# Agent attention with a gated convolution on one core: loads without a hold, twelve query units transposed by TensorE, another order of TensorE's steps

## The chip, the core and the metric

The kernel runs on one core of one Trainium2 chip, in one launch. The metric is the device time of that core in microseconds: the median of 3 runs of the kernel before is 424.46 us (422.56 to 425.1).

## What is computed

Four batches of 12800 rows and 128 channels, 49 agents per batch, all float32 at the interface. `sm` is a softmax over the last axis.

```python
a2k = sm(agents, k)              # scale = 1/sqrt(128) inside sm
agent_v = a2k @ v                # 49 x 128 per batch
x = sm(q, agents) @ agent_v      # 12800 x 128 per batch
gate_pre[:, s] = sum(conv_w[j] * xp[:, s + j] for j in range(5))   # xp: x with 4 zero rows ahead
out = (sigmoid(gate_pre) * (x @ w_val)) @ w_out
```

## The kernel before

**Units.** A batch is cut into 10 units of 1280 rows, so there are 40 units of k, 40 of v and 40 of q, and the query units are numbered 0 to 39 through all batches (unit 21 is q2.1). The output is cut into 25 chunks of 512 rows per batch, chunk 0 to 100 (the last 512 rows are two half chunks). Two query units make a segment of 2560 rows, which five chunks read: segment 11 is units 22 and 23, and chunk 55 is the first that reads it.

**Steps on TensorE.** `k` (a unit's key scores) and `q` (its query scores) are 16 fp32 matmuls of 320 columns each (L404). `v` multiplies a unit's exponentials with v, 40 fp32 matmuls of 129 columns (20 of 64 weights' columns in batch 0; L508). `t` transposes a query unit's weights. For a chunk there are `g` (five fp16 matmuls at L950 on the rows x1, and a sixth at L954 on x2), `a` (L977, L981) and `o` (three, L1020 to L1022), each of 512 columns. `m` and `f` are the few small steps that take a batch's maximum and fold its agent values with the weights of the gate, the value and the output. The text `order` (L1065 on) is a list of all these steps written out by hand, and TensorE does its steps in that order. Four PSUM accumulators stand beside it: two banks `sc`, in turn for k, q and the t that TensorE does, and one each for gate, val and out.

**A query unit's way.** After `q`, VectorE transposes in 32x32 blocks (L414, sT) and takes the maximum (L773), GpSimd subtracts it (L778, qw), ScalarE exponentiates (L786), VectorE sums, inverts and scales (L791, L792, L795, L800), and ScalarE (L807) and GpSimd (L813, L821) write the fp16 weights and their rests, `pt`, 128 rows by 10 blocks of 128. `pt` is one of 4 buffers. A transpose then brings `pt` into x1: units 0 to 3 by TensorE (ten transposes at L876, then ScalarE copies one half out of PSUM at L883 and VectorE the other at L888), the other 36 by a DMA transpose on SyncE's queue (L862). Two further DMAs per segment (L911, x<-x, of 60 and 35 rows) copy shifted rows of x1 into x2, once both units stand in x1.

**The DMA queue.** All loads, DMA transposes, x<-x copies and output stores are issued by SyncE, in one order, and each waits there for what it needs before the next is issued. A load (L397) takes one of 11 buffers `ld` in turn, so the load of a unit needs the buffer that the unit 11 places earlier in the list of k, v and q steps has used. Eight DMA semaphores are used in turn: a DMA is issued when the eighth before it has landed.

**The planner.** Every step is recorded with an engine, a planned duration, what it reads and writes (`Plan.add`, L79), and `Plan.order` (L92) replays the whole in a cost model and returns the order in which the instructions are emitted: on TensorE the order of the text, on the other engines and on the queue the ready step with the longest chain behind it. It replays twice. From the first replay it takes when the first user of each load starts, and in the second a load is held until HOLD = 13 us (planned) before that (`early`, L398; `hold`, L101).

Of the kernel before, what the change touches and what calls it, by code (L numbers as in the profile page):

```python
# [44 lines left out]
CUT = 2  # L45
NOB = 4
SINGLE = 4
PE_FIRST = 4
PE_TURNS = ()
TURN = 3  # L50
W_AT = 2
HOP = 0.07
GAP = {"act": 0.11, "dve": 0.1, "pool": 0.055}
SWITCH = 0.13
DRAIN = 0.16
LANES = 8
FIRST = 0.85
LAND = 0.95
MEET = 0.3
HOLD = 13.0  # L60
BEGIN = {"pe": 1.5, "act": 2.4, "dve": 1.6, "pool": 2.3, "dma": 1.2}

QS = 256.0
# [4 lines left out]
class Plan:  # L68
# [7 lines left out]
    def __init__(self):  # L76
        self.steps, self.wrote, self.read = [], {}, {}

    def add(self, engine, us, fn, reads=(), writes=(), moved=0.0, key=None, urge=0.0, early=None):  # L79
        i = len(self.steps)  # L80
        need = set()
        for x in reads:
            need |= self.wrote.get(x, set())
        for x in writes:
            need |= self.wrote.get(x, set()) | self.read.get(x, set())
        for x in reads:
            self.read.setdefault(x, set()).add(i)
        for x in writes:
            self.wrote[x], self.read[x] = {i}, set()
        self.steps.append((engine, us, fn, need, moved, key, urge, early))  # L90

    def order(self):  # L92
        self.replay({})
        users = {i: [] for i, s in enumerate(self.steps) if s[7] is not None}
        for j, s in enumerate(self.steps):
            for i in s[3]:
                if i in users:
                    users[i].append(self.start[j])
        return self.replay({i: min(users[i]) - self.steps[i][7] for i in users})

    def replay(self, hold):  # L101
        n = len(self.steps)
        after = [[] for _ in range(n)]
        last = None
# [6 lines left out]
                last = i  # L111
        tail = [0.0] * n
        for i in reversed(range(n)):
            engine, us, fn, need, moved, key, urge, early = self.steps[i]
            cost = us + HOP
            if engine == "dma":
                cost = FIRST + moved + LAND
            tail[i] = cost + urge + max((tail[j] for j in after[i]), default=0.0)
        engines = ("pe", "act", "dve", "pool", "dma")
        free = dict(BEGIN)  # L120
        wire = 0.0
        lanes = [0.0] * LANES
        left = [len(s[3]) for s in self.steps]
        at = [hold.get(i, 0.0) for i in range(n)]
        queues = {e: [] for e in engines}
        pe = [i for i, s in enumerate(self.steps) if s[0] == "pe"]
        here = 0
# [5 lines left out]
        done = 0  # L133
        while done < n:
            best = None
            free["dma"] = max(free["dma"], lanes[0])
            for e in engines:
                if e == "pe":
                    if here < len(pe) and not left[pe[here]]:
                        pick, when = pe[here], max(free[e], at[pe[here]])  # L140
                    else:
                        continue
                elif queues[e]:
                    q = queues[e]
                    soon = min(max(free[e], at[i]) for i in q)
                    open_ = [i for i in q if at[i] <= soon + 0.05]
                    pick = max(open_, key=lambda i: (tail[i], -i))
                    for i in q:
                        if tail[i] > tail[pick] + 1.0 and at[i] < soon + 0.6 * self.steps[pick][1]:
                            pick = i  # L150
                    when = max(free[e], at[pick])
                else:
                    continue
                if best is None or when < best[0]:
                    best = when, e, pick
            when, e, i = best
            engine, us, fn, need, moved, key, urge, early = self.steps[i]
            if e == "pe":
                here += 1
                if key != kind and {key, kind} & {"sc", "av"}:  # L160
                    when += SWITCH
                kind = key
                end = when + us + DRAIN + HOP
                free[e] = when + us
            elif e == "dma":
                queues[e].remove(i)
                free[e] = when + us
                busy = wire > when + FIRST
                wire = max(wire, when + FIRST) + moved
                if key == "t":  # L170
                    wire += MEET if busy else 0.0
                    free[e] = max(free[e], wire - moved)
                end = wire + LAND
                lanes = lanes[1:] + [end]
            else:
                queues[e].remove(i)
                end = when + us + HOP
                free[e] = when + us - GAP[e]
            start[i] = when
            done += 1  # L180
            for j in after[i]:
                if i in self.steps[j][3]:
                    left[j] -= 1
                    at[j] = max(at[j], free[e] if e == "pe" == self.steps[j][0] else end)
                    if not left[j] and self.steps[j][0] != "pe":
                        queues[self.steps[j][0]].append(j)
# [5 lines left out]
def tile_agent_attention_gated_conv(  # L192
# [10 lines left out]
    B, C, N = qT.shape  # L203
    A = 49
    NU = N // UNIT
# [11 lines left out]
    add = plan.add  # L217
# [8 lines left out]
    m2 = const.tile([P, 2], F32, name="m2")  # L226
# [155 lines left out]
    def load(kind, b, u):  # L382
        i = taken[0] % NLOAD
        taken[0] += 1
        slot_of[kind, b, u] = i
        if kind == "v":
            dst, src = ld[i], vP[b, u].rearrange("p n c -> p (n c)")
        else:
            dst = ld[i][:, 0:UNIT]
            src = (kT if kind == "k" else qT)[b, :, u * UNIT : (u + 1) * UNIT]  # L390
# [4 lines left out]
        for d, f, keys in parts:  # L395
            add(
                "dma", 0.46, lambda d=d, f=f: nc.sync.dma_start(out=d, in_=f), (), keys,  # L397
                1.65 * f.shape[1] / src.shape[1], early=HOLD,  # L398
            )

    def score_matmuls(b, src, out):
# [426 lines left out]

    def on_pe(b, u):
        g = b * NU + u  # L830
        return g < PE_FIRST or (g < (B - 1) * NU and g % TURN in PE_TURNS)

    def unit_rows(g):
        o = PAD + g % 2 * UNIT
# [224 lines left out]
    def step(fn, b):  # L1059
# [3 lines left out]

    kinds = {"m": "max", "f": "fold"}
    order = (  # L1065
# [24 lines left out]
    )  # L1090
    work = [(kinds.get(x[0], x[0]), *map(int, x[1:].split("."))) for x in order.split()]

# [67 lines left out]
```

## Time and profile before

| what | value |
|---|---|
| median of 3 runs | 424.46 us |
| the profiled execution | 428.87 us |
| its span, first to last instruction | 426.9 us |
| TensorE busy | 398.2 us, 93% of the span |
| VectorE, ScalarE, GpSimd busy | 305.1, 305.8, 236.5 us |
| share of the SP queue's packets in 16 DMA engines' span | 94.1% |
| DMA packets moved | 127.64 MB |

A busy TensorE counts modelled ends of pipelined matmuls, so the time of a step is read from the start of one to the start of the next. The DMA share is the time of all packets over that of 16 engines, and goes over 1 where packets of several DMAs are under way on an engine at once. Waits are put down to what came last.

### The profile page before, as it was taken

What the parts mean: (1) busy time and instruction counts of PE and PEld (TensorE: products, weight loads), DVE (VectorE), ACT (ScalarE), POOL (GpSimd) and SP (SyncE); (2) the same over time, 40 slices, a digit from 0 to 9 for tenths busy, and PEclk for the clock granted to TensorE, in tenths of its full rate; (3) what the DMA queues carried; (4) which work ended last, traced back from release to release, by engine and by line L of the source; (5) the groups of instructions that cost most, each with busy time, mean ns of one, the idle gap of its engine ahead of it and who ended that gap; (6) DMA issues with size and microseconds to landing.
All of it is one profiled execution on the core that took longest, in us unless ns stands there. A gap on an engine that the chain in (4) does not pass through costs nothing.

```text
span 426.9 us, 10123 instructions
## 1 busy us (share of the span) xinstructions
PE 398.2 (93%) x3907; PEld 199.7 (47%) x3907; DVE 305.1 (71%) x570; ACT 305.8 (72%) x524; POOL 236.5 (55%) x303
## 2 busy tenths in 40 slices
PE   5869989997999999999989999999989999999996
PEld 2329534455454443464734444446564444444443
DVE  5988879776887778569658978486475887777221
ACT  7657347895658767997648677689826778778876
POOL 2510236454467635755756455674462879886653
PEclk9998999999999999999999999999998999999999
DMA  8999997999999999999999999979999778496733
GB/s 320 419 370 415 391 323 243 343 349 418 318 258 283 340 325 228 371 405 232 399 231 350 346 348 280 267 267 319 343 388 219 249 209 288 96 335 201 205 134 138
DMA packets 75131, 127.64 MB, mean 299 GB/s; under 512 B 50466, under 2 KB 50978, under 8 KB 75084
## 3 DMA queue, kind: packets, MB, share of 16 engines
q1 hardware_dynamic: 74940, 126.87, 94.1%
q8 instruction: 31, 0.51, 0.5%
q10 hardware_dynamic: 144, 0.13, 0.2%
q14 instruction: 16, 0.13, 0.1%
HBM read 79.25 MB, written 26.21 MB: 247 GB/s over the span
## 4 chain that ended last, share of the span: by engine, by line
PE 56%; DMA 35%; DVE 4%; ACT 2%; issue 2%; SPq 1%; POOL 0%; ACTq 0%; DVEq 0%
PE gate L950 18%; DMA ld<-kT 16%; PE sc L404 11%; DMA x<-pt 8%; DMA ld<-vP 5%; PE val L977 4%; PE out L1020 4%; DMA x<-x 4%; PE val L981 4%; PE out L1021 4%; PE gate L954 4%; PE out L1022 4%; DMA ld<-qT 3%; PE av L508 3%; DVE h L990 1%
## 5 line engine op out<-in xcount | busy, mean ns | idle before, releaser
L1001 POOL TENSOR_TENSOR hl<-h,hh 128x512 f16<-128x512 f32 (+1 forms) x101 | 117.4, 1167 | 89.1 <-ACT hh L996 87.1
L950 PE MATMUL gate<-x,stat 128*128 128x512 f16 (+1 forms) x500 | 124.1, 378 | 0.7 <-ACT th L963 0.5
L990 DVE SCALAR_TENSOR_TENSOR h<-th,val 128x512 f32<-128x512 f32 x100 | 67.7, 677 | 69.6 <-PE val L981 35.7
L404 PE MATMUL sc<-ld,ag_sb 128*32 128x320 f32 x1280 | 99.4, 444 | 12.0 <-DMA ld<-qT 7.2
L963 ACT ACTIVATE th<-gate,unscale 128x512 f32<-128x512 f32 x100 | 68.3, 683 | 34.9 <-PE gate L954 33.0
L1034 ACT ACTIVATE ob<-out,oscale 128x512 f32<-128x512 f32 x98 | 67.2, 686 | 14.5 <-PE out L1022 14.3
L950 PEld LDWEIGHTS <-stat 128*128 128x128 f16 x505 | 48.4, 98 | 59.9 <-issue 6.3
L996 ACT CAST hh<-h 128x512 f16<-128x512 f32 (+1 forms) x101 | 61.5, 611 | 18.4 <-DVE h L990 17.2
L404 PEld LDWEIGHTS sc<-ld,ag_sb 128*32 128x32 f32 x1280 | 38.9, 111 | 62.2 <-issue 13.2
L778 POOL TENSOR_TENSOR qw<-sT,qmx 128x490 f32<-128x490 f32 x40 | 40.6, 1020 | 29.1 <-DVE qmx L773 28.7
L508 PE MATMUL av<-ld,eT 128*32 128x129 f32 (+1 forms) x1400 | 49.6, 276 | 4.8 <-DVE eT L414 2.4
L508 PEld LDWEIGHTS av<-ld,eT 128*32 128x32 f32 (+1 forms) x1400 | 46.2, 115 | 9.9 <-DVE eT L414 3.9
L813 POOL TENSOR_SCALAR pt<-qw 128x240 f16<-128x240 f32 x80 | 28.1, 373 | 31.8 <-DVE qw L800 31.8
L821 POOL TENSOR_TENSOR pt<-qw,pt 128x490 f16<-128x490 f32 x40 | 43.6, 1094 | 3.3 <-ACT pt L807 3.3
L497 ACT ACTIVATE e<-ks,kbias 128x320 f32<-128x320 f32 x80 | 39.4, 554 | 6.5 <-DVE eT L414 6.1
L414 DVE STREAM_TRANSPOSE sT<-sc 128x640 f32<-128x640 f32 x40 | 33.6, 844 | 13.9 <-PE sc L404 12.7
L430 ACT COPY ks<-sc 128x640 f32<-128x640 f32 x40 | 27.4, 689 | 21.8 <-PE sc L404 19.2
L414 DVE STREAM_TRANSPOSE eT<-e 128x640 f32<-128x640 f32 x40 | 33.3, 839 | 12.6 <-PE av L508 7.6
L954 PE MATMUL gate<-x,stat 128*128 128x512 f16 x100 | 38.0, 380 | 3.7 <-DMA x<-x 3.7
L977 PE MATMUL val<-x,stat 128*128 128x512 f16 x100 | 38.1, 381 | 1.4 <-DVE h L990 1.3
L981 PE MATMUL val<-x,stat 128*128 128x512 f16 x100 | 38.0, 380 | 0.0
L1020 PE MATMUL out<-hh,wo 128*128 128x512 f16 x98 | 37.5, 383 | 0.0
(133 smaller groups left out, 428.4 us busy)
## 6 DMA issues: line engine op xcount, KB each, us to landing
ld<-qT SPq DMA_DIRECT2D x40, 640.0 KB
ld<-kT SPq DMA_DIRECT2D x40, 640.0 KB
ld<-vP SPq DMA_DIRECT2D x39, 645.0 KB
outT<-ob SPq DMA_DIRECT2D x48, 512.0 KB
x<-x SPq DMA_DIRECT2D x18, 300.0 KB
x<-x SPq DMA_DIRECT2D x18, 175.0 KB
outT<-ob SPq DMA_DIRECT2D x3, 256.0 KB
x<-x SPq DMA_DIRECT2D x4, 150.0 KB
```

What stands on the lines that cost most here:

```text
L404: nc.tensor.matmul(out=out[g * BLK : (g + 1) * BLK, j, 0:GT], lhsT=ag_sb[:, b, j * BLK : (j + 1) * BLK], rhs=src[:, g * GT : (g + 1) * GT] ...
L414: nc.vector.transpose(out=out.rearrange("p n (j i) -> p j n i", j=2), in_=in_.rearrange("p j (n i) -> p j n i", i=BLK),)
L508: nc.tensor.matmul(out=av[o + j : o + j + cols, 0 : C + 1], lhsT=et[:, n, j : j + cols], rhs=vt[:, n, :], start=(u == 0 and n < 2), stop=( ...
L950: nc.tensor.matmul(out=pg, lhsT=stat[:, k, :], rhs=x1[:, c : c + w], start=(k == 0), stop=False,)
L954: nc.tensor.matmul(out=pg, lhsT=stat[:, TAPS + 1, :], rhs=x2[:, o2 : o2 + w], start=False, stop=True,)
L963: lambda: nc.scalar.activation(out=th, in_=pg, func=AF.Tanh, scale=unscale[:, 0:1]),
L977: nc.tensor.matmul(out=pv, lhsT=stat[:, TAPS, :], rhs=x1s[(b * NCH + n0 // CH) // 5 % NX][:, PAD + o2 : PAD + o2 + w], start=True, stop=False,
L981: nc.tensor.matmul(out=pv, lhsT=stat[:, TAPS + 2, :], rhs=x2[:, o2 : o2 + w], start=False, stop=True,)
L990: lambda: nc.vector.scalar_tensor_tensor(out=h, in0=th, scalar=1.0, in1=pv, op0=ALU.add, op1=ALU.mult),
L996: "act", 0.19 + 0.42 * scale, lambda: nc.scalar.copy(out=hh, in_=h),
L1001: lambda: nc.gpsimd.tensor_tensor(out=hl, in0=h, in1=hh, op=ALU.subtract),
L1034: lambda: nc.scalar.activation(out=ob[:, o : o + w], in_=po, func=AF.Copy, scale=oscale),
```

## The change

Three things change. First, the hold: `early`, the first replay and `hold` are gone, so a load may be ordered as soon as its buffer is free; in place of the hold the cost model issues no DMA while the transfers already issued would take more than BACKLOG = 2.5 us (planned) from then. Nothing of BACKLOG is in the emitted program but the order. Second, TensorE also transposes units 6, 9, 12, 15, 18, 21, 24 and 27, beside 0 to 3; the queue has 28 DMA transposes instead of 36. Third, the text of TensorE's steps is another one. In it the k, v and q steps stand in 27 runs (before: 29) between fp16 steps, counting a `t` of TensorE as fp16.

```diff
-PE_FIRST = 4
-PE_TURNS = ()
-TURN = 3
+PE_UNITS = (0, 1, 2, 3) + tuple(range(6, 28, 3))
...
+BACKLOG = 2.5
...
-HOLD = 13.0
...
     def order(self):
-        self.replay({})
-        users = {i: [] for i, s in enumerate(self.steps) if s[7] is not None}
-        for j, s in enumerate(self.steps):
-            for i in s[3]:
-                if i in users:
-                    users[i].append(self.start[j])
-        return self.replay({i: min(users[i]) - self.steps[i][7] for i in users})
-
-    def replay(self, hold):
...
-        at = [hold.get(i, 0.0) for i in range(n)]
+        at = [0.0] * n
...
-            free["dma"] = max(free["dma"], lanes[0])
+            free["dma"] = max(free["dma"], lanes[0], wire - BACKLOG)
...
-                1.65 * f.shape[1] / src.shape[1], early=HOLD,
+                1.65 * f.shape[1] / src.shape[1],
...
-        return g < PE_FIRST or (g < (B - 1) * NU and g % TURN in PE_TURNS)
+        return g in PE_UNITS
...
-        "o5 a8 t0.7 k2.1 v1.2 v1.3 k2.2 v1.4 v1.5 k2.3 v1.6 q0.9 o6 g11 o7 a9 t0.8 t0.9 g12 a10 "
-        "o8 k2.4 q1.0 o9 a11 q1.1 q1.2 v1.7 v1.8 v1.9 o10 a12 g13 a13 f1 o11 g14 a14 t1.0 t1.1 "
+        "g16 o11 a14 g17 q1.1 v1.2 v1.3 q1.2 t1.1 v1.4 q1.3 k2.1 v1.5 v1.6 v1.7 v1.8 v1.9 k2.2 "
+        "k2.3 o12 a15 g18 t1.2 o13 a16 f1 g19 o14 a17 f1 g20 o15 a18 g21 o16 k2.4 k2.5 k2.6 k2.7 "
...
+        "g39 o34 a37 g40 t1.9 q2.1 v2.8 k3.3 v2.9 q2.2 o35 t2.0 a38 g41 o36 f2 a39 t2.1 g42 o37 "
```

Lines after the first are 11 lower in the changed kernel (L404 is L393, L414 is L403, L862 is L851, L911 is L900).

Place one, SyncE's queue around the DMA transpose of unit 23 (q2.3; it reads pt3 and writes x1_3) and the x<-x copies of segment 11 (they write x22, which is x2 buffer 2). Before:

```order
L862 DMA_TRANSPOSE x1_3_104<-pt2_99 128x10x128
L911 DMA x21_106<-x1_2_103 60x1x2560
L911 DMA x21_106<-x1_2_103 35x1x2560
L862 DMA_TRANSPOSE x1_3_104<-pt3_100 128x10x128
L1049 DMA outT<-ob1_121 128x1024
L397 DMA ld8_69<-qT 128x1280
L911 DMA x22_107<-x1_3_104 60x1x2560
L397 DMA ld9_70<-qT 128x1280
L911 DMA x22_107<-x1_3_104 35x1x2560
```

And in the changed kernel:

```order
L1038 DMA outT<-ob2_122 128x1024
L386 DMA ld10_71<-qT 128x1280
L386 DMA ld0_61<-qT 128x1280
L386 DMA ld1_62<-qT 128x1280
L386 DMA ld2_63<-vP 128x1290
L386 DMA ld3_64<-vP 128x1290
L386 DMA ld4_65<-vP 128x1290
L386 DMA ld5_66<-vP 128x1290
L851 DMA_TRANSPOSE x1_3_104<-pt3_100 128x10x128
L386 DMA ld6_67<-vP 128x1290
L386 DMA ld7_68<-vP 128x1290
L900 DMA x22_107<-x1_3_104 60x1x2560
```

Seven loads (q2.8 to v3.3) now stand straight ahead of that transpose and two more between it and the copies; before, none of the three places ahead of it was a load, and one load stood ahead of the copies.

Place two, VectorE between the block transpose (sT1) and the scaling (qw1) of unit 21, the unit whose `t2.1` TensorE now does. Before:

```order
L414 STREAM_TRANSPOSE sT1_86<-sc0_134 128x2x10x32
L414 STREAM_TRANSPOSE sT0_85<-sc1_135 128x2x10x32
L990 SCALAR_TENSOR_TENSOR h2_113<-th2_110,val_137 128x512
L773 TENSOR_REDUCE qmx1_88<-sT1_86 128x10
L773 TENSOR_REDUCE qmx0_87<-sT0_85 128x10
L990 SCALAR_TENSOR_TENSOR h0_111<-th0_108,val_137 128x512
L990 SCALAR_TENSOR_TENSOR h1_112<-th1_109,val_137 128x512
L791 TENSOR_REDUCE qsm1_94<-qw1_90 128x10
L792 SCALAR_TENSOR_TENSOR qsm1_94<-qsm1_94,tiny_146 128x10
L795 RECIPROCAL qr1_96<-qsm1_94 128x10
L990 SCALAR_TENSOR_TENSOR h2_113<-th2_110,val_137 128x512
L800 TENSOR_TENSOR qw1_90<-qw1_90,qr1_96 128x490
```

And in the changed kernel:

```order
L403 STREAM_TRANSPOSE sT1_86<-sc0_134 128x2x10x32
L762 TENSOR_REDUCE qmx1_88<-sT1_86 128x10
L780 TENSOR_REDUCE qsm0_93<-qw0_89 128x10
L781 SCALAR_TENSOR_TENSOR qsm0_93<-qsm0_93,tiny_146 128x10
L784 RECIPROCAL qr0_95<-qsm0_93 128x10
L789 TENSOR_TENSOR qw0_89<-qw0_89,qr0_95 128x490
L536 COPY av2_165<-av_139 128x129
L780 TENSOR_REDUCE qsm1_94<-qw1_90 128x10
L781 SCALAR_TENSOR_TENSOR qsm1_94<-qsm1_94,tiny_146 128x10
L784 RECIPROCAL qr1_96<-qsm1_94 128x10
L789 TENSOR_TENSOR qw1_90<-qw1_90,qr1_96 128x490
```

The maximum of unit 21 now follows its transpose at once, and what stands between is the scaling of unit 20 (qw0) and the copy of a batch's agent values, in place of four steps of chunks (h) and another unit's two.

## Rows read from the trace of the kernel before

**Rows 1.** The page: span, and section 1 (busy us, share of the span, instructions).

```profile
span 426.9 us, 10123 instructions
PE 398.2 (93%) x3907; PEld 199.7 (47%) x3907; DVE 305.1 (71%) x570; ACT 305.8 (72%) x524; POOL 236.5 (55%) x303
```

**Rows 2.** Busy time of each engine in stretches (start:end, length, then busy us and instructions of PE, PEld, DVE, ACT, POOL; the last three columns are granted clock, DMA share, GB/s).

```profile
40.00:420.00 380.00, 367.46 (x3554) 182.27 (x3551) 273.10 (x512) 274.64 (x478) 224.32 (x279) 1.00 0.95 292
20.00:40.00 20.00, 15.05 (x202) 10.85 (x196) 16.12 (x31) 13.34 (x26) 1.83 (x4) 0.91 1.02 392
60.00:80.00 20.00, 18.88 (x158) 8.15 (x159) 16.23 (x27) 14.07 (x24) 12.28 (x15) 1.00 0.90 279
320.00:340.00 20.00, 18.88 (x106) 8.48 (x106) 12.80 (x31) 13.26 (x23) 10.04 (x13) 0.91 0.90 228
```

**Rows 3.** What TensorE waited for between 40 and 420 us (waiting line, releaser: us in total, times, longest).

```profile
PE gate L954 <- DMA x<-x: 3.7, 2, 3.0
PE av L508 <- DMA ld<-vP: 2.4, 4, 1.2
PE sc L404 <- DMA ld<-qT: 1.9, 4, 1.0
PE sc L404 <- DMA ld<-kT: 1.8, 3, 1.1
```

**Rows 4.** The time line, TensorE: its first scores, the ten v of batch 0, and its first gate matmuls (start, us, what; in brackets the idle time before and what ended it).

```profile
5.28 8.19 PE L404 MATMUL sc<-ld,ag_sb 128*32 128x320 f32 x80 [5.28 <-DMA ld<-qT]
...
32.58 12.90 PE L508 MATMUL av<-ld,eT 128*64 128x129 f32 x200 [2.42 <-DVE eT L414]
...
52.31 1.24 PE L950 MATMUL gate<-x,stat 128*128 128x512 f16 x5
```

**Rows 5.** The same between 84 and 94 us: fp16 steps, then v, two k, v, a q, then fp16 again.

```profile
85.15 0.38 PE L954 MATMUL gate<-x,stat 128*128 128x512 f16 x1
85.46 1.31 PE L508 MATMUL av<-ld,eT 128*32 128x129 f32 x40
86.58 2.34 PE L404 MATMUL sc<-ld,ag_sb 128*32 128x320 f32 x32
88.73 1.29 PE L508 MATMUL av<-ld,eT 128*32 128x129 f32 x40
89.83 1.26 PE L404 MATMUL sc<-ld,ag_sb 128*32 128x320 f32 x16
91.03 0.39 PE L1020 MATMUL out<-hh,wo 128*128 128x512 f16 x1
...
91.69 0.38 PE L977 MATMUL val<-x,stat 128*128 128x512 f16 x1
...
92.12 1.25 PE L950 MATMUL gate<-x,stat 128*128 128x512 f16 x5
...
93.42 0.38 PE L1020 MATMUL out<-hh,wo 128*128 128x512 f16 x1
```

**Rows 6.** The time line at the last `t` of TensorE, and two groups by line, TensorE's transposes and ScalarE's copies of them (busy us, mean ns of one, idle time before).

```profile
63.61 0.72 PE L876 MATMUL sc<-ident,pt 128*128 128x128 f16 x10
64.17 0.38 PE L977 MATMUL val<-x,stat 128*128 128x512 f16 x1
L876 PE MATMUL sc<-ident,pt 128*128 128x128 f16 x40 | 2.9, 219 | 0.9 <-POOL pt L821 0.7 <-ACT ks L430 0.2
L883 ACT COPY x<-sc 128x640 f16<-128x640 f16 x4 | 2.8, 691 | 0.9 <-PE sc L876 0.9
```

**Rows 7.** The time line of query unit 0 from its block transpose to TensorE's transposes.

```profile
7.69 0.85 DVE L414 STREAM_TRANSPOSE sT<-sc 128x640 f32<-128x640 f32 x1 [2.08 <-PE sc L404]
...
15.71 0.56 PEld L876 LDWEIGHTS <-pt 128*128 128x128 f16 x10 [1.27 <-POOL pt L821]
```

**Rows 8.** The DMAs: sizes by kind, and the DMA transposes as instructions on SyncE's queue (duration ns min/median/max, first and last start us).

```profile
ld<-kT SPq DMA_DIRECT2D x40, 640.0 KB
outT<-ob SPq DMA_DIRECT2D x48, 512.0 KB
x<-x SPq DMA_DIRECT2D x18, 300.0 KB
x<-x SPq DMA_DIRECT2D x18, 175.0 KB
L862 SPq DMA_TRANSPOSE x<-pt x36: 1342/2772/8391, 70.5 to 398.4; - x36
```

**Rows 9.** TensorE's time line at two of its waits for loads, q0.9 and q2.2.

```profile
106.86 1.28 PE L404 MATMUL sc<-ld,ag_sb 128*32 128x320 f32 x16 [0.23 <-DMA ld<-qT]
...
216.36 1.28 PE L404 MATMUL sc<-ld,ag_sb 128*32 128x320 f32 x16 [0.28 <-DMA ld<-qT]
```

**Rows 10.** SyncE's queue and TensorE around the longest wait for x<-x (segment 13, chunk 65).

```profile
298.97 5.08 SPq L862 DMA_TRANSPOSE x<-pt  x1
304.18 1.62 SPq L397 DMA_DIRECT2D ld<-vP  x3
305.90 1.28 SPq L1049 DMA_DIRECT2D outT<-ob  x2
309.09 1.69 SPq L911 DMA_DIRECT2D x<-x  x2
...
321.12 0.59 PE L954 MATMUL gate<-x,stat 128*128 128x512 f16 x1 [2.95 <-DMA x<-x]
```

More of the change, by code (lines that the diff above doesn't have):

```diff
@@ L77, in __init__, with add @@
         self.steps, self.wrote, self.read = [], {}, {}
-    def add(self, engine, us, fn, reads=(), writes=(), moved=0.0, key=None, urge=0.0, early=None):
+    def add(self, engine, us, fn, reads=(), writes=(), moved=0.0, key=None, urge=0.0):
         i = len(self.steps)
@@ L89, in add @@
             self.wrote[x], self.read[x] = {i}, set()
-        self.steps.append((engine, us, fn, need, moved, key, urge, early))
+        self.steps.append((engine, us, fn, need, moved, key, urge))
     def order(self):
-        self.replay({})
-        users = {i: [] for i, s in enumerate(self.steps) if s[7] is not None}
-        for j, s in enumerate(self.steps):
-            for i in s[3]:
-                if i in users:
-                    users[i].append(self.start[j])
-        return self.replay({i: min(users[i]) - self.steps[i][7] for i in users})
-    def replay(self, hold):
         n = len(self.steps)
@@ L113, in replay @@
         for i in reversed(range(n)):
-            engine, us, fn, need, moved, key, urge, early = self.steps[i]
+            engine, us, fn, need, moved, key, urge = self.steps[i]
             cost = us + HOP
@@ L156, in replay @@
             when, e, i = best
-            engine, us, fn, need, moved, key, urge, early = self.steps[i]
+            engine, us, fn, need, moved, key, urge = self.steps[i]
             if e == "pe":
```

43 rows, old and new, of the table order are left out of this document.

## The prediction

> **What bounds the kernel now.** I read the page first. TensorE is busy 93% of a span of 426.9 us, VectorE and ScalarE a little over 70% [rows 1]; so what TensorE waits for decides. The stretches come next: between 40 and 420 us TensorE is busy 367.46 of 380 us, which leaves 12.5 us idle, at a DMA share of 0.95 [rows 2]. Two things are full at once, and the question is what a relief of the queue gives back against what it costs TensorE.
>
> The list of waits says what ends the idle time: DMAs, 3.7 us for x<-x, 2.4 for v, 1.9 for q, 1.8 for k, together 9.8 of the 12.5 [rows 3]. After the 2.95 us wait for x<-x the granted clock is 0.91 over 320 to 340 us, where it is 1.00 before [rows 2, 10]: 0.09 of 20 us, 1.8 us more. So DMAs cost 11.6 us after the start, 6.1 for loads and 5.5 for x<-x.
>
> **Prices on TensorE.** From start to start a score step is 1.075 us (two in 2.15), v 1.10, g 1.30, a 0.43, o 0.66; entering an fp32 run costs 0.09 (0.31 from the last fp16 matmul, of which the matmul is 1.30/6), leaving one 0.12, together 0.21 [rows 5]. A v of batch 0 is 1.29 (ten in 12.90) [rows 4], a t of ten transposes 0.56 [rows 6]. The small steps m and f I put at 0.2 and 0.3. With these I can say how much work of its own TensorE has done ahead of any step, and compare it with its start: the first gate starts at 52.31 us [rows 4] after 35.8 us of work (17 scores, ten v, three t, six runs, some small steps), so TensorE trails its work by 16.5 us by then.
>
> **Prices in the queue.** A load is 640 KB, an output 512, the two x<-x of a segment 475 [rows 8]; in the stretch of 20 to 40 us, nearly all loads, 392 GB/s flow [rows 2]. That makes 1.67, 1.34 and 1.24 us. A DMA transpose has no such row: as an instruction on the queue it takes 1.34 us at least, 2.77 at the median [rows 8]. The minimum belongs to an empty queue and this one is full, so I take 2.77.
>
> **Why loads are late, and whether they still will be.** I add up what the queue has to move up to a load, and set it against TensorE's work ahead of the step that uses it. Before, q0.9: 51 loads, 2 transposes, 5 x<-x pairs (four of them of one unit, half as long) and 2 outputs make 97.1 us, against 85.3 us of work; the queue is 11.8 behind. It starts at 106.86 [rows 9], 21.6 behind its work, so a load is usable some 9.8 us later than the tally. q2.2: 85 loads, 13 transposes, 10 pairs and 15 outputs make 207.3, against 189.8; 17.5 behind. It starts at 216.36 [rows 9], 26.6 behind, so 9.1 later than the tally. The two agree. After the change the worst place past the start is k2.3, at the end of a run of 14 fp32 steps: 58 loads, 3 transposes, 6 pairs, 5 outputs, 116.9 us, against 109.9 of work. It asks for a trail of 7.0 + 9.8 = 16.8 us, and TensorE trails by about 16.5 from the start on. At q2.2, 87 loads, 10 transposes, 11 pairs and 16 outputs make 205.0, against 200.8: a trail of 14.0. So the order, more than the eight transposes, takes the loads' waits away, because chunks stand ahead of the scores that they used to follow. I take all 6.1 us; at worst none is saved.
>
> **x<-x.** The queue has one order, so a transpose waits behind loads that go out in a burst. Before, the transpose at 298.97 had three v loads and two outputs between it and its x<-x copies at 309.09, and these let TensorE go on at 321.12 [rows 10]. The hold had kept those loads back until that burst. Without it the burst comes where fp32 steps free buffers. At segment 11 seven loads (11.7 us), the transpose (2.77), two more loads (3.3) and the copies (1.24) follow the end of q2.3, 19.0 us, with 2.9 us more as the first load shows (first scores at 5.28, queue from 0.74 on, less 1.67) [rows 4]: 21.9, where TensorE has 25.2 us of steps up to chunk 55 (11 scores, five g, six a, five o, a t). At segment 14 eight loads, two transposes, an output and the copies, 21.5 + 2.9 = 24.4, stand against 25.7 from the end of v3.0 on (nine v, two scores, five g, six a, six o). I call both about even: half of the 5.5 us is saved, 2.75; the ends are all of it and none.
>
> **What TensorE gets.** Eight t more: 8 x 0.56 = 4.5 us. Two fp32 runs less, 29 to 27: -0.4. A t also waits for pt, with all of TensorE behind it. Unit 0 needs 8.0 us from its block transpose to TensorE's transposes, in a stage with little else, and TensorE's weight load had been idle 1.27 us for it [rows 7]. TensorE's own steps between q and t give 8.2 us for unit 21 and 9.4 for unit 27, the shortest, and 11 to 22 for the others; VectorE now scales unit 20 between, and does four h less. Ends: 0, and 8 x 1.27 = 10.2. I take 2.0, a wait at units 21 and 27 and little else.
>
> The copies out of PSUM, 0.69 us on ScalarE for each t [rows 6] and a like one on VectorE, I price at 0: both engines are idle over a quarter of the span [rows 1], and a unit's first chunk is 11 us or more behind its t. With that cover gone they would cost 8 x 0.69 = 5.5.
>
> **The start.** Loads of q0.3 and k1.0 now stand ahead of v0.9's, 2 x 1.67 = 3.3 us later, while TensorE does two scores and one t more ahead of its first gate, 2.7 us. I take 0; the ends are -2.7 and 3.3.
>
> **Sum.** 4.5 - 0.4 + 2.0 - 6.1 - 2.75 = -2.75 us. The profiled execution's span of 426.9 becomes 424.15. Its own time is 428.87, 2.0 over the span; the median is 4.4 us under that. Applied to the median, 424.46 - 2.75 = **421.7 us**.
>
> **A rule against the change.** Ten transposes of TensorE took 0.72 us together, the next matmul starting 0.56 after the first of them, and the granted clock of that stretch is 1.00 [rows 2, 6]. The Trainium skill, page "TensorE: Matmul & The Clock Gate", section "Part 4: PE-mode transpose", says a 128x128 transpose takes about 275 ns in a kernel, and that the clock's full rate does not engage for it. By that rule 80 more would be 22.0 us instead of 4.5, and the time 439.2. The trace does not agree with it: neither the spacing nor the clock shows it.
>
> **Rivals.**
> *x<-x late twice.* Both bursts jam as segment 13 did: 2 x (2.95 + 1.8) = 9.5 us in place of my 2.75, so 421.7 + 6.75 = 428.5, slower than before. It decides where a segment's copies land over 25.2 us after q2.3 (25.7 for segment 14). For it: one queue, and my margins of 3.3 and 1.3 us. Against: the copies are needed only by a gate's sixth matmul, 1.08 us on.
> *TensorE waits for pt.* All eight new t wait like the first one did: 10.2 instead of 2.0, so 429.9. For it: pt takes 8.0 us even in an empty stage. Against: six units have over 11 us, and the order on VectorE now favours these units.
> *The queue was the bound.* Both x<-x waits go and no t waits: -2.75 - 2.0 more, so 417.0. For it: the DMA share of 0.95. Against: burst places remain.
> *Transposes don't overlap.* Each costs the 219 ns of its own record [rows 6], 80 x 0.219 = 17.5 instead of 4.5, so 434.7. Against it stands the spacing of 56 ns.
>
> **Chances.** A measurement of this kernel can tell about 1% from no change: 420.2 to 428.7. Forecast 0.50, itself from 418.5 to 425, of which 0.18 lies under 420.2. Queue as the bound 0.19, all faster. x<-x late 0.17, of which 0.08 over 428.7 and the rest within 1%. pt late 0.13, 0.10 over. No overlap 0.01. Faster 0.18 + 0.19 = 0.37; slower 0.08 + 0.10 + 0.01 = 0.19; the rest, 0.44, within 1%. The range of 414.5 to 429.5 leaves out the low end of the queue's case (0.04) and the upper ends of the two late ones and the last (0.13).
>
> **What would show it.** TensorE's waits for ld loads after 40 us under 1 us in all; for x<-x two or three short ones at segments 11 and 14; at L865 idle time from GpSimd's pt near 2 us, most of it at units 21 and 27; DMA transposes 28; a DMA share under 0.95. I am wrong if loads still make TensorE wait for over 3 us (then the tally misses what blocks the queue), if the first gate starts over 3 us later than 52.31 with only the 2.7 us of work gained, or if ScalarE and VectorE take the place of the DMAs in the list of waits.

## The result and the profile after

The changed kernel takes 428.54 us (median of 20 runs, 425.55 to 432.39), the kernel before 425.15 us in the runs beside it (20 runs, 422.56 to 430.63). The ratio is 1.0079, with a 95% interval of 1.0058 to 1.0099: 0.8% slower, where 421.7 us, 0.65% faster, was forecast. The profiled executions took 432.35 us here and 428.87 before, each 3.7 to 3.8 us over its kernel's median.

The page of the changed kernel and its stretches, in the columns of [rows 1, 2] (start:end, length, busy us and instructions of PE, PEld, DVE, ACT, POOL, then granted clock, DMA share, GB/s):

```profile
span 430.6 us, 10315 instructions
PE 402.5 (93%) x3987; PEld 207.5 (48%) x3987; DVE 306.7 (71%) x578; ACT 311.3 (72%) x532; POOL 237.2 (55%) x303
...
q8 instruction: 31, 0.51, 0.5%
```

```profile
40.00:420.00 380.00, 366.37 (x3580) 186.71 (x3577) 274.44 (x521) 276.13 (x480) 222.12 (x275) 0.99 0.91 284
300.00:320.00 20.00, 15.65 (x403) 12.32 (x401) 11.77 (x20) 12.45 (x24) 6.19 (x8) 1.00 0.90 319
320.00:340.00 20.00, 18.17 (x116) 9.45 (x116) 15.53 (x38) 11.15 (x20) 11.35 (x15) 0.91 0.57 161
```

The span is 3.7 us longer. TensorE is idle for 13.6 us between 40 and 420, as it was before (12.5), although the DMA share has gone from 0.95 to 0.91. What it waits for is another thing, as its waits in that stretch show (us in total, times, longest):

```profile
PE av L497 <- issue: 9.7, 5, 3.0
PE gate L939 <- ACT th L952: 2.4, 6, 0.7
PE sc L393 <- DMA ld<-qT: 0.3, 1, 0.3
```

Against [rows 3], loads fall from 6.1 to 0.3 us and x<-x from 3.7 to nothing. In their place stand 9.7 us put down to "issue": nothing that the profile shows held TensorE. In the kernel before that was this line alone:

```profile
PE sc L404 <- issue: 0.2, 1, 0.2
```

All five are inside runs of v. The time line of v3.0 to v3.9, ten in a row, on TensorE:

```profile
304.47 3.73 PE L497 MATMUL av<-ld,eT 128*32 128x129 f32 x128
309.48 3.73 PE L497 MATMUL av<-ld,eT 128*32 128x129 f32 x127 [1.28 <-issue]
314.77 3.72 PE L497 MATMUL av<-ld,eT 128*32 128x129 f32 x126 [1.56 <-issue]
321.00 0.74 PE L497 MATMUL av<-ld,eT 128*32 128x129 f32 x18 [2.51 <-issue]
```

The breaks come every 126 to 128 matmuls. Each matmul has a weight load of its own, so that is some 256 instructions, and the page has a queue q8, kind "instruction": 31 packets of together 0.51 MB for 2 x 3987 = 7974 instructions of TensorE, 257 to a packet. At 1.10 us for 80 instructions a packet lasts 3.5 us; from break to break it took 5.0, 5.3 and 6.2. Ten v took 17 us instead of 11. The DMA view of 302 to 322 us has three such packets beside the loads (packets, MB, share of the 16 engines):

```profile
q1 hardware_dynamic: 1417, 6.32, 87.8%
q8 instruction: 3, 0.05, 0.8%
```

The single records of the trace tie the breaks to these packets. Ahead of the five breaks stand 2753, 4545, 6337, 6593 and 6849 records of TensorE, each 193 more than a multiple of 256, and each break ends 1.3 to 1.5 us after a packet of q8 has ended. In the rows above TensorE enters a block of 256 at 304.47 and is through with it after 3.7 us; the next packet starts 2.7 us after that entry and takes 0.9, and TensorE goes on 1.4 after its end: 5.0 us together.

The rest is near what was worked out. The first gate comes 1.87 us after its place in [rows 4], and a new t still costs 0.56 us to the next start:

```profile
54.18 1.25 PE L939 MATMUL gate<-x,stat 128*128 128x512 f16 x5
...
230.63 0.73 PE L865 MATMUL sc<-ident,pt 128*128 128x128 f16 x10
231.19 1.24 PE L939 MATMUL gate<-x,stat 128*128 128x512 f16 x5
```

The account of the span: -9.5 for loads and x<-x, +9.5 for issue (it was 0.2 before), +4.1 for work of TensorE's own (8 x 0.56 less 0.4); +4.1 against 3.7 measured. Waits for ScalarE and VectorE are not in it: those for th are 1.9 longer, those for h 1.3 shorter.

### The profile page after: what moved, and what is told of

Its sections match the earlier page's. It is cut to its first block, busy times and chain, and to the rows that moved or that the text cites. A ratio compares the mean times of both kernels' runs of the same rounds, so it can differ in the third digit from the quotient of the medians.

```text
span 430.6 us, 10315 instructions
## 1 busy us (share of the span) xinstructions
PE 402.5 (93%) x3987; PEld 207.5 (48%) x3987; DVE 306.7 (71%) x578; ACT 311.3 (72%) x532; POOL 237.2 (55%) x303
## 4 chain that ended last, share of the span: by engine, by line
PE 72%; DVE 11%; DMA 7%; ACT 5%; issue 4%; POOL 1%; SPq 0%; DVEq 0%; ACTq 0%
PE gate L939 20%; PE sc L393 16%; PE av L497 11%; DMA ld<-qT 5%; PE out L1009 4%; PE val L966 4%; PE gate L943 4%; PE val L970 4%; PE out L1011 4%; PE out L1010 4%; DVE h L979 2%; ACT th L952 2%; DVE qsm L780 1%; DVE qw L789 1%; DVE qsm L781 1%
## 5 line engine op out<-in xcount | busy, mean ns | idle before, releaser
L990 POOL TENSOR_TENSOR hl<-h,hh 128x512 f16<-128x512 f32 (+1 forms) x101 | 119.0, 1185 | 80.3 <-ACT hh L985 76.4
L393 PE MATMUL sc<-ld,ag_sb 128*32 128x320 f32 x1280 | 99.4, 450 | 7.8 <-DMA ag_sb<-agT 6.0
L1023 ACT ACTIVATE ob<-out,oscale 128x512 f32<-128x512 f32 x98 | 67.2, 686 | 14.1 <-PE out L1011 13.6
L393 PEld LDWEIGHTS sc<-ld,ag_sb 128*32 128x32 f32 x1280 | 41.0, 112 | 54.1 <-issue 9.4
L497 PE MATMUL av<-ld,eT 128*32 128x129 f32 (+1 forms) x1400 | 52.0, 284 | 12.1 <-issue 9.7
L497 PEld LDWEIGHTS av<-ld,eT 128*32 128x32 f32 (+1 forms) x1400 | 47.8, 118 | 18.0 <-issue 12.6
L403 DVE STREAM_TRANSPOSE sT<-sc 128x640 f32<-128x640 f32 x40 | 33.7, 845 | 21.5 <-PE sc L393 20.3
L403 DVE STREAM_TRANSPOSE eT<-e 128x640 f32<-128x640 f32 x40 | 33.1, 834 | 18.0 <-PE av L497 10.7
L796 ACT CAST pt<-qw 128x490 f16<-128x490 f32 x40 | 23.9, 599 | 18.6 <-DVE qw L789 14.1
```

Of the source, the lines that this page charges most:

```text
L393: nc.tensor.matmul(out=out[g * BLK : (g + 1) * BLK, j, 0:GT], lhsT=ag_sb[:, b, j * BLK : (j + 1) * BLK], rhs=src[:, g * GT : (g + 1) * GT] ...
L403: nc.vector.transpose(out=out.rearrange("p n (j i) -> p j n i", j=2), in_=in_.rearrange("p j (n i) -> p j n i", i=BLK),)
L497: nc.tensor.matmul(out=av[o + j : o + j + cols, 0 : C + 1], lhsT=et[:, n, j : j + cols], rhs=vt[:, n, :], start=(u == 0 and n < 2), stop=( ...
L990: lambda: nc.gpsimd.tensor_tensor(out=hl, in0=h, in1=hh, op=ALU.subtract),
L1023: lambda: nc.scalar.activation(out=ob[:, o : o + w], in_=po, func=AF.Copy, scale=oscale),
```

## The experiments

The theory after the result, "instructions": in a long run of v TensorE uses its instructions up faster than packets of them arrive while the queue is full, and the changed order has longer runs of v (ten in a row in batch 3, eight in a run of 14 steps in batch 1, seven in a run of 12 in batch 2; before, five in a row at most in these batches; a `t` that the DMA does is no step of TensorE). Its first rival, "data": a wait without a name is a wait for loads all the same. The second, "t": the eight transposes cost what was lost.

**Fewer instructions for the same v.** 64 columns of weights per matmul make a v of 20 matmuls, as batch 0 has it.

```diff
-        cols = BLK if b else AP_
+        cols = AP_
```

In the changed kernel:

> The changed kernel with each v step of batches 1 to 3 as 20 matmuls of 64 weight columns instead of 40 of 32, as batch 0 has it: the same loads, the same order, half the instructions. Theory 'instructions' (in a long run of v steps TensorE uses up its 256 instructions of 16 KB in 3.7 us and waits for the next 16 KB): the five waits at L497 put down to issue (9.7 us) vanish, and 30 v steps cost 1.29 instead of 1.10 us, 5.7 us more; 428.5 - 9.7 + 5.7 = about 424.5, down to 420 if what the waits cost in the clock goes too. Rival 'data' (the waits are for v loads or for transposed exponentials, wrongly put down): nothing but the 5.7 us changes, about 434, and the waits stay.

In the kernel before:

> The same edit on the kernel before, whose longest runs have five v steps and which shows no wait of this kind at its v steps. Both theories: 5.7 us more, about 431; it is the price of the edit.

Changed: 421.36 us, ratio to the kernel before 0.9904 (0.9870 to 0.9937). Its page and its longest waits of TensorE from 40 to 420 us:

```profile
q8 instruction: 26, 0.43, 0.5%
```

```profile
PE gate L939 <- ACT th L952: 2.5, 6, 0.7
PE gate L943 <- DMA x<-x: 1.6, 1, 1.6
```

No issue wait of a v is left, with the same v, loads and order; that is against "data". The ten v of batch 3 run through, 1.12 us each:

```profile
301.39 11.24 PE L497 MATMUL av<-ld,eT 128*64 128x129 f32 x200
312.55 2.36 PE L393 MATMUL sc<-ld,ag_sb 128*32 128x320 f32 x32
```

Before: 421.36 us too, 0.9911 (0.9884 to 0.9938), where 431 was expected. That miss has two parts. I had priced a v of 64 columns by [rows 4], 1.29, which is a stage with other limits; in the v64_no_t trace below a single v starts 1.25 us ahead of the next step, and ten in a row take the 1.12 above. And the waits for loads and x<-x fell there from 9.8 to 1.9 us, though the edit moves no load. They had not been instructions: of the waits of 0.15 us and more in the trace of before, only that of 0.2 us put down to issue stands at the edge of a block of 256 records. Nor does TensorE just ask later: q0.9 waits for its load there too, and starts at 105.56 us instead of 106.86 [rows 9]. Why loads came earlier, these two runs don't say.

**The long run by itself, in the kernel before.** v3.0 to v3.9 in one run; nothing else is changed in the text, and the planner's orders on the queue and the other engines follow from it.

```diff
-q2.8 v3.0 v3.1 v3.2 q2.9 t2.8 v3.3 v3.4 g62 t2.9 ... q3.0 q3.1 v3.5 v3.6 v3.7 t3.0 v3.8 v3.9
+q2.8 q2.9 t2.8 g62 t2.9 ... q3.0 q3.1 v3.0 v3.1 v3.2 v3.3 v3.4 v3.5 v3.6 v3.7 t3.0 v3.8 v3.9
```

> The kernel before with the ten v steps of batch 3 in one run. Theory 'instructions': three waits put down to issue appear in that run, 127 matmuls apart, 1.3 to 2.8 us each, some 6 us in all: 429 to 432. Rival 'data': no such wait, at most waits for v loads: 424 to 428.

433.04 us, 1.0173 (1.0131 to 1.0215), and its first wait is the new one:

```profile
PE av L508 <- issue: 7.2, 3, 2.6
```

Two of the three, 4.6 us, stand in the new run; three were expected there. So the order of the steps is enough for such waits, with the hold and the transposes of before. The third, 2.6 us, ends at 122.39 us in batch 1, where the text is that of before: the packet started 6.9 us after TensorE had entered the block, and what kept it is not shown.

**The long runs cut.** The changed kernel, with chunks put between its long runs of v, three v at most in a row.

```diff
-v1.5 v1.6 v1.7 v1.8 v1.9 k2.2 k2.3 o12 a15 g18 t1.2 o13 a16 f1 g19
+v1.5 v1.6 o12 a15 g18 v1.7 v1.8 t1.2 o13 a16 g19 v1.9 k2.2 k2.3 f1
...
-v3.0 v3.1 v3.2 v3.3 v3.4 v3.5 v3.6 v3.7 v3.8 v3.9 t2.9 t3.0 q3.1 q3.2 o59 a62 g65 f3
+v3.0 v3.1 v3.2 o59 a62 g65 v3.3 v3.4 v3.5 t2.9 o60 a63 g66 v3.6 v3.7 v3.8 t3.0 o61 a64 g67
```

> The changed kernel with its three long runs of v steps cut by chunk steps into pieces of at most three v. Theory 'instructions': at most one short wait of this kind is left, 9.7 us and the 1.8 us of slow clock are saved, four more fp32 runs cost 0.9: 417 to 420. Rival 'data': the waits move or stay, within 1% of 428.5.

425.83 us, 1.0001 (0.9969 to 1.0034), where 417 to 420 was expected. The issue waits of v are gone, and others came:

```profile
PE gate L939 <- ACT th L952: 3.6, 9, 0.7
PE gate L939 <- ACT hh L985: 2.0, 1, 2.0
PE sc L393 <- issue: 1.5, 1, 1.5
```

The 2.0 us put down to hh are instructions too: that hh had ended 0.4 us before the gate went on, the place is 6593 records from the start again, and a packet of q8 had ended 1.2 us before. So of 9.7 us, 3.5 are left, at a score and a gate; the waits for th grew by 1.2, and six more fp32 runs at 0.21 cost 1.3. That leaves 3.7; the ratios differ by 0.8%, 3.3 us. In the traces of all kernels here, each of TensorE's waits of 0.15 us and more that is put down to issue, from 40 to 420 us, stands at such an edge of a block, and ends 1.3 to 1.7 us after a packet.

**A long run where nothing else moves.** Behind the last chunk of the changed kernel, 12 v of 32 weight columns and 12 of 64, on data already there.

```diff
     for i in plan.order():
         plan.steps[i][2]()
+    et, vt = ets[0], ld[0].rearrange("p (n c) -> p n c", c=C + 1)
+    for cols in (BLK, AP_):
+        for u in range(12):
+            for n in range(NBLK):
+                o = (n % 2) * AP_
+                for j in range(0, AP_, cols):
+                    nc.tensor.matmul(out=av[o + j : o + j + cols, 0 : C + 1], ...)
```

> The changed kernel, and behind its last chunk 12 v of 32 weight columns (13.2 us of work) and then 12 v of 64 columns (about 14 us), in a stage where the queue has only the last outputs to move. If the instructions come late because the DMA engines are full of loads, no issue wait over 0.5 us shows there. If a packet of 256 instructions takes longer than 128 such matmuls last whatever else moves, two or three waits of 1.3 to 3 us stand in the first half, and none in the second.

The time line of all 24 on TensorE and of the weight loads of the first 12, the stretch of these and its packets:

```profile
423.44 27.50 PE L1112 MATMUL av<-ld,eT 128*32 128x129 f32 x720
428.36 3.52 PEld L1112 LDWEIGHTS av<-ld,eT 128*32 128x32 f32 x128 [0.28 <-issue]
432.09 3.52 PEld L1112 LDWEIGHTS av<-ld,eT 128*32 128x32 f32 x128 [0.21 <-issue]
435.82 1.48 PEld L1112 LDWEIGHTS av<-ld,eT 128*32 128x32 f32 x55 [0.21 <-issue]
```

```profile
424.00:438.00 14.00, 13.91 (x478) 13.10 (x472) 0.00 (x0) 0.02 (x1) 0.00 (x0) 1.00 0.16 55
```

```profile
q8 instruction: 4, 0.07, 2.0%
```

720 matmuls without a wait that the time line shows: 950 instructions in 14 us, four packets, all only just in time, for the weight loads still break at each block's edge, by 0.21 to 0.28 us. A packet starts here 1.0 to 1.6 us after TensorE has entered a block; ahead of the changed kernel's five breaks it was 2.7 to 4.8. Once started it takes about as long in both, 0.9 to 1.4 us here and 0.9 to 1.1 there. In the same trace the run of ten v near 310 us has two such waits, 1.3 and 2.2 us. So length of the run alone doesn't do it; the packet starts late where the engines are also full (0.90 to 0.97 there, 0.16 here). These shares are means: ahead of the first of the three breaks shown above, from 304.47 to 308.20 us, it was 0.64. The other compute engines rest in the tail too, so that it is the engines' load is the likeliest reading, not one isolated by this run.

**The change taken apart.** Each of these has some of its three parts. order_only is the kernel before with the changed order's text. units_only is the kernel before with this edit, and hold_kept is units_only with the changed text:

```diff
-        return g < PE_FIRST or (g < (B - 1) * NU and g % TURN in PE_TURNS)
+        return g in PE_UNITS
```

no_t is the changed kernel with this one, and hold_off_only is no_t with the old text:

```diff
-PE_UNITS = (0, 1, 2, 3) + tuple(range(6, 28, 3))
+PE_UNITS = (0, 1, 2, 3)
```

> The kernel before with the changed kernel's order of TensorE's steps, hold and 36 DMA transposes kept. If TensorE's instructions are the cause (waits marked issue inside the long runs of v), the runs of v are those of the changed kernel and 6 to 10 us of such waits appear: 427 to 432 us. If the eight t are the cause of the loss, it is gone without them: 421 to 425 us.

> The kernel before with units 6 to 27 by threes transposed by TensorE, in the old order and with the hold. The t cost 8 x 0.56 = 4.5 us of TensorE, and the runs of v stay at five at most, so no issue wait over 1 us inside a run of v. If the queue's relief (eight DMA transposes less) takes the 6.1 us of load waits away, as the prediction had it: 423 to 426 us. If the load waits were not the queue's, or TensorE then waits for pt: 428 to 434 us.

> The kernel before with its order and units, and without the hold (the cost model's bound on transfers under way in its place). If loads were late because they were held: 418 to 421 us, with load waits under 1 us after 40 us. If they were late because of what the queue has to move, or if the wait was for instructions all along: 424 to 428 us, with load waits where they were.

> The changed kernel with only units 0 to 3 transposed by TensorE, at 32 weight columns. With 64 columns the eight t were worth 7 to 8 us although they cost TensorE 4.5. If that is the queue (loads, x<-x and outputs behind eight more DMA transposes), it is the same here, and the instruction waits come on top: 433 to 438 us, with a wait for x<-x or for ScalarE held by an output. If at 32 columns TensorE's time is lost to instructions anyway, the queue's delay is hidden: 426 to 430 us.

> The changed kernel's order and units with the hold of the kernel before. If bursts of unheld loads are what delays the instruction packets, the issue waits inside the runs of v shrink below 5 us, and the time is 424 to 428 us. If the length of the runs decides, 8 to 10 us of them stay, loads are waited for again (the 6 us of the kernel before), and it is 431 to 436 us.

| order | eight t | hold | name | us | ratio to before (95%) |
|---|---|---|---|---|---|
| old | no | yes | before | 425.15 to 426.84 | 1 |
| old | no | no | hold_off_only | 425.51 | 0.9976 (0.9948 to 1.0004) |
| old | yes | yes | units_only | 442.95 | 1.0394 (1.0354 to 1.0435) |
| new | no | yes | order_only | 442.57 | 1.0380 (1.0334 to 1.0426) |
| new | no | no | no_t | 436.56 | 1.0250 (1.0184 to 1.0316) |
| new | yes | yes | hold_kept | 442.00 | 1.0345 (1.0295 to 1.0395) |
| new | yes | no | changed | 428.54 | 1.0079 (1.0058 to 1.0099) |

Each ratio is to the kernel before in runs beside it (425.15 us for the last, 426.02 to 426.84 for the others). The eighth combination, the old order with the eight t and no hold, was not run. order_only, units_only and hold_kept came out 6 to 11 us over the top of what was expected. The parts don't add: the order costs 2.7% without the hold and 3.8% with it, and the two others make it bearable. Waits of TensorE in order_only and then in hold_kept:

```profile
PE av L508 <- issue: 6.8, 4, 4.5
PE gate L954 <- DMA x<-x: 4.4, 1, 4.4
PE av L508 <- DMA ld<-vP: 2.5, 7, 0.8
```

```profile
PE av L506 <- issue: 11.7, 5, 2.9
PE gate L952 <- DMA x<-x: 4.5, 2, 3.3
```

With the hold back, instructions are later still (11.7 us). So it isn't the missing hold that makes them late, as the first case of hold_kept's expectation has it. In units_only, where the old order has its t close behind its q, two t wait for pt, the longer one for 7.86 us:

```profile
80.08 1.25 PE L874 MATMUL sc<-ident,pt 128*128 128x128 f16 x10 [7.86 <-POOL pt L819]
81.26 1.30 PE L402 MATMUL sc<-ld,ag_sb 128*32 128x320 f32 x8
```

```profile
80.08:81.26 1.18, 1.18 (x11) 0.98 (x11) 0.00 (x0) 0.00 (x0) 0.00 (x0) 0.50 0.88 235
```

That is the prediction's rival of the late pt, in a kernel that was not the changed one. After such a wait the t takes 1.18 us to the next start at a granted clock of 0.50 (1.2 GHz), where it took 0.56 in a busy stretch at 1.00 (2.4 GHz).

**What the eight t are worth.** no_t against the changed kernel is 1.7%, 7.3 us in favour of the t; so I asked the same with the instructions out of the way.

> The changed kernel with 64 weight columns in every v, and with only units 0 to 3 transposed by TensorE. With the supply of instructions out of the way, it stands against the same with the eight t, 421.4 us. If the queue has room for eight more DMA transposes in this order, their 4.5 us of TensorE are gained: 416 to 418 us. If it has not, loads and x<-x make TensorE wait for as much as the t cost: 420 to 424 us.

429.61 us, 1.0069 (1.0029 to 1.0108), against 0.9904 with the t: again 1.7%, where 416 to 424 was expected. The t are worth more than the 4.5 us that they cost. The longest wait that comes without them, on SyncE's queue, then ScalarE, then TensorE:

```profile
181.19 8.19 SPq L386 DMA_DIRECT2D ld<-vP  x5
190.62 0.34 SPq L1038 DMA_DIRECT2D outT<-ob  x1
193.54 4.24 SPq L851 DMA_TRANSPOSE x<-pt  x1
```

```profile
202.29 0.69 ACT L1023 ACTIVATE ob<-out,oscale 128x512 f32<-128x512 f32 x1 [4.41 <-DMA outT<-ob]
202.88 0.69 ACT L419 COPY ks<-sc 128x640 f32<-128x640 f32 x1
```

```profile
193.68 1.32 PE L497 MATMUL av<-ld,eT 128*64 128x129 f32 x20
194.93 1.28 PE L393 MATMUL sc<-ld,ag_sb 128*32 128x320 f32 x16
...
197.40 2.36 PE L393 MATMUL sc<-ld,ag_sb 128*32 128x320 f32 x32
203.62 2.24 PE L393 MATMUL sc<-ld,ag_sb 128*32 128x320 f32 x16 [3.86 <-ACT ks L419]
```

An output's store stands behind the loads of five v and has a transpose at its heels; ScalarE waits 4.41 us for the buffer `ob` that it is to free, the copy of a score out of PSUM stands behind that on ScalarE, and TensorE waits 3.86 us for the PSUM bank. No row of that chain names TensorE's wait a DMA. It is not the whole loss: from 40 to 420 us TensorE waits 9.2 us for th and ks here and 2.5 with the t, and for x<-x not at all instead of 1.6. That is 5.1 us more, and the t's 4.5 are saved, where the two profiled executions (426.43 and 421.89 us) are 4.5 apart. Where the rest goes is not shown.

**Where the hold's gain went.** hold_off_only has no waits for loads, and is only 0.24% faster, with an interval that holds no change. Second profiles of three kernels:

> The kernel before, unchanged, for a second profile. If its waits for loads are a property of its order (the prediction's 6.1 us), they are there again, 4 us or more. If they came with one slow execution, they are mostly gone: under 2 us.

> The kernel before without the hold, for a second profile; the first was of an execution of 420.7 us, where the median is 425.5. If what it loses in most executions is instructions or ScalarE, waits marked issue, ks or ob of 3 us or more show here that the first profile did not have. Loads under 1 us again.

> The changed kernel for a second profile. If its instruction waits belong to its runs of v, they stand at the same places (124, 209, 308 to 318 us), 6 to 11 us in all.

Before again (426.3 us, span 424.4), then the hold off again (423.78 us, span 421.6), TensorE's longest waits:

```profile
PE sc L404 <- DMA ld<-qT: 2.6, 4, 1.3
PE av L508 <- DMA ld<-vP: 2.4, 4, 1.5
PE gate L954 <- DMA x<-x: 1.7, 1, 1.7
PE sc L404 <- DMA ld<-kT: 1.3, 4, 0.4
```

```profile
PE sc L393 <- ACT ks L419: 2.4, 2, 1.7
PE gate L943 <- DMA x<-x: 2.0, 4, 1.4
```

The 6.3 us for loads belong to the kernel before. Without the hold they are gone, and 4.4 us stand there for ks and x<-x, where x<-x had 1.7. The two profiles of the hold off have spans 2.8 and 5.8 us under that of before again; 0.24% is 1.0 us. Both are of executions under their kernel's median of 425.51 us (423.78 and 420.73, its shortest), so they show more than the median has. The changed kernel again (431.13 us) has 8.7 us of issue in v, four times, at its three long runs.

**Both gains at once.** The kernel before without the hold and with 64 columns:

> The kernel before with its order and units, without the hold, and with 64 weight columns in every v. If the two gains are apart from each other (the hold's 0.24 percent and the 0.9 percent of the v), they add: 420 us or less where the kernel before has 426. If both took away the same waits, it is no faster than with the v alone: 421 to 423 us.

422.73 us, 0.9943 (0.9907 to 0.9979): they don't add. v64_changed and v64_before, 421.36 us each, are the shortest of all kernels run, 0.9% under the kernel before.

## Why the prediction was wrong

**What failed** is "What TensorE gets", and the price behind it: "v 1.10", read from single v between other steps, and taken for every v in whatever run. The changed order was counted there as "two fp32 runs less, 29 to 27: -0.4". It has a term that is not in the sum, 9.5 us more waiting for instructions, and with it the sum of -2.75 becomes +6.75. x<-x came out 0.95 us better than its term, pt 2.0 better and the loads 0.3 worse, which makes the 4.1 of the account above; the profiled span is +3.7. None of the rivals has it, and none of the signs under "What would show it" would have. That the time is that of one rival, 428.5, is chance: its x<-x waits are not there. Without that term, at 64 columns in both kernels, the change makes no difference that these runs show (421.36 and 421.36), so the forecast 2.75 us are not seen there either.

The trace of before could have warned: q8 stands on its page with the same 31 packets, though only 0.2 us of waits stand at their edges. The Trainium skill, page "Runtime: NRT & Kernel Launch", section "Instruction fetch mechanics", says that instructions come in 16 KiB blocks of 256 and that crossing into the next one is mostly hidden. The first agrees with these runs (31 packets, 257 each; breaks at multiples of 256 records). The second holds for the tail, at 0.21 to 0.28 us, and not in a long run of v in a full queue, at 1.28 to 3.0 us a break.

**Loads: right that they go, wrong about why and what for.** "All 6.1" went to 0.3. But "the order, more than the eight transposes" doesn't do it: order_only still waits 5.2 us for loads (2.5 for v, 1.8 for k, 0.9 for q), while units_only, in the old order with the hold, waits 0.9, though TensorE is held up by pt there, and hold_off_only doesn't wait for them at all. And the saving was priced as if nothing stood behind it: without the hold alone it comes to 1.0 us, not clear of noise.

**x<-x: better than forecast.** Half of it was to go, all went. With the hold in the new order it is 4.4 and 4.5 us in one or two waits (order_only, hold_kept). That loads which go out early leave the queue free there is likely, but no run shows it alone.

**The t: right in price, wrong in sign.** 0.56 each is measured, and pt, for which 2.0 us were taken, holds two of the weight loads up after 40 us, 0.8 us in all, and no matmul. But the new order needs them: without them the time is 7.3 us longer, and an output is late and ScalarE with it, which is a part of that. The prediction held that against no term at all; it looked at loads and x<-x in the queue, and not at outputs.

**The start: right**, 1.87 us later with 2.7 us more work ahead.

**What stays open:** what keeps a packet from starting, why loads come earlier in v64_before, and where the rest of the 7.3 us goes that the eight t are worth.

## What to carry to other kernels

Count TensorE's instructions, not only its columns: where a step has small matmuls with a weight load each, read how long one instruction packet lasts in it (instructions by the packets of the page's instruction queue), and see if a full DMA queue can bring the next in that time: here 3.5 us in v, where the next came after 5.0 to 6.2. Half as many matmuls for the same work took these waits away; fp16 steps of 512 columns between left a third. A wait for instructions is known by its place, a multiple of 256 records from the others, more than by its name: hh in runs_cut was one. An order of steps, its units and its queue's rule are one design: the order or the units alone cost 4% here, the order with one of the other two 2.5 to 3.5%, all three 0.8%; the hold's removal alone costs nothing.

## What was not expected of the hardware

- Instruction packets in a full queue: a block of 256 instructions took 5.0 to 6.2 us from break to break where its work is 3.5, because its packet started 2.7 to 4.8 us after TensorE had entered the block before; in a quiet queue it started after 1.0 to 1.6, and four came in 14 us with breaks of 0.3 us at most.
- The same ten transposes take 0.56 us to the next start in a busy stretch at a granted clock of 1.00, and 1.18 at 0.50 after TensorE was idle for 7.86 us.
- An output's store that is late behind loads stops TensorE through ScalarE, with 4.41 us on ScalarE and 3.86 on TensorE.
